# Attention, gated FFN and routed experts on one core: probabilities scaled two units ahead, biases written by ScalarE, first weights converted inside attention

## The chip, the cores and the metric

The kernel runs on one core of one Trainium2 chip. The metric is the device time of one execution in microseconds (us), the median of several runs; lower is better. Before the change it is 889.53 us, the median of 3 runs between 889.01 and 889.55.

## The reference

What has to be computed, cut to what matters here (B, H, S, D = 4, 8, 576, 64):

```python
scores = q @ k.transpose(0, 1, 3, 2) / sqrt(D)
rel = pos[:, None] - pos[None, :]
mask = (rel >= 0) & (rel < 128)                     # a window of 128 keys
scores = where(mask, scores - slopes[h] * abs(rel), -1e9)   # a bias of its own for each head
attn = exp(scores - scores.max(-1));  attn /= attn.sum(-1) + 1e-9
x = (attn @ v) as 2304 tokens x 512

gate = 1 / (1 + exp(-(x @ w_gate)))                 # w_gate, w_val: 512 x 1536, float64
x = gate * (x @ w_val) @ w_out                      # w_out: 1536 x 512, float64

# then every token goes to one of 8 experts (relu FFN, 512 -> 1024 -> 512), times its gate
```

The result is float32. In the FFN the kernel splits each operand into a high part (a copy in the type fp32r) and the rest, and adds three products (high x high, high x low, low x high).

## The kernel before

**Units of attention.** 18 blocks of 128 tokens are cut into chunks of 2, 4, 4, 4 and 4 blocks. A unit is two heads times two blocks of queries; there are 36. Each unit passes through four functions:

- `unit_s`: TensorE multiplies queries with keys into two PSUM banks (line 216). For each head and block VectorE adds the bias and takes the row's minimum in one instruction (226; the score is kept negated), and ScalarE writes exponentials and their row sum (229).
- `unit_n`: VectorE forms the reciprocals of the four sums (239, 240). Four instructions scale the probabilities by them (`scale_rows`, 108): on GpSimd, but for units 0 and 1 every second one on VectorE.
- `unit_t`: TensorE transposes the scaled probabilities (256), and VectorE and ScalarE copy them to SBUF (`hi_copy`).
- `unit_b`: TensorE multiplies them with the values (289), and the result is copied into the tile `xf` of the chunk.

`bias_of` (148) writes a head's bias, 128 x 256, the first time that it is asked for; `make_edge` copies a bias and puts a large negative number where a block holds the border of a batch. Both run on GpSimd.

**The first loop** (units 0 to 20, `NA = 20`) stands in a stretch whose order on TensorE, VectorE and ScalarE is that of the code; GpSimd's order is left to the scheduler. In pass i the code makes the edges of unit i+5, transposes unit i, scales unit i+1, multiplies unit i-1 with its values and asks for the scores of unit i+3. The table `AT` adds further work to single passes: loading the FFN's first weights, converting them, and building the operands of its token side.

**Operands of the FFN.** The FFN's two input products run as a scheme of seven products for two pairs of chunks of 512 tokens (`PAIRS`), with sums and differences of blocks in place of the eighth; the first 256 tokens (`rest`) run plainly. The token side needs A11, A12, A22 and S1 to S4. `S1+` and its like form a sum (`sum_x`, 305), and `S1` and its like split an operand: ScalarE casts the high part (96), VectorE subtracts it (112). The weight side comes in 12 blocks f. `load_w` fetches the float64 words, `conv_w` turns them into float32 (ScalarE 116, VectorE 122 to 125), `sum_w` forms four differences (354 to 357), and `split_w` casts and subtracts as above, once for the four blocks of weights (z = 0) and once for the four differences (z = 1). Converted weights go to DRAM too, from where `load_wt` fetches them for the second pair.

**The second loop** (units 20 to 35) fixes the order of TensorE alone. Between the parts of a unit it runs steps of the first pair's products, 9 for each block f (m1 to m7, and rg and rv of the rest columns), as many in a unit as `STEPS` says. Each step is followed by a part of the next block's conversion: `after` loads block f+2 behind m1, and behind later steps converts, differences and splits block f+1. Block 0's own `sum_w` and `split_w` stand ahead of the loop (530, 531, 534), with A12 and S4.

**The seam and the second pair.** What is left of the first pair's steps runs four at a time, and after each four one operand of the second pair is built (`seam`). Then the second pair's weights of block 0 are split, and S2, S3, A22 and S4 are built between its first products. In each of its blocks `split_wo(f)` also converts a block of the output weights, which come in use in the next stage. Operands, weights and converted weights all live in one pool `bpool` of 33 tiles (`slot`); a tile comes free when its last reader is done. A second pool, `op_`, of 8 tiles of the same size, is opened when attention's pool is closed, and holds the output weights.

Of the kernel before, what the change touches and what calls it, by code (L numbers as in the profile page):

```python
# [10 lines left out]
F32R = mybir.dt.float32r  # L11
# [4 lines left out]
ALU = mybir.AluOpType  # L16
# [32 lines left out]
UB = 5  # L49
STEPS = [2, 3, 4, 4] + [5] * 12  # L50


@with_exitstack
def attn_ffn_moe(ctx: ExitStack, tc: tile.TileContext, qd, kd, vd, wgv, w_out, emb, tau, w1, w2, cst, ids, out):
# [93 lines left out]
    def bias_of(h):  # L148
        while len(bias_t) <= h:
            z = len(bias_t)  # L150
            if z % 4 == 0:
                bias_c.append(slot([P, 4, 256], F32, f"bias{z}"))
            t = bias_c[-1][:, z % 4, :]
            nc.gpsimd.tensor_scalar(out=t, in0=relm, scalar1=-8.0 * 2.0 ** (-8.0 * (z + 1) / H), scalar2=0.0,
                                    op0=ALU.mult, op1=ALU.add)
            bias_t.append(t)
        return bias_t[h]
# [203 lines left out]
    def load_wt(f):  # L361
        if f < KF:
            for z, (d, src) in enumerate(((wf, wf_d), (tf, tf_d))):
                d[f] = slot([P, 2 * KD, P], F32, f"wt{z}_{f}")
                nc.sync.dma_start(flat(d[f]), src[f * P:(f + 1) * P, :])

    def split_w(pair, f, z):
        if f < KF:
            t = (wf, tf)[z].pop(f)
            h_, l_ = (slot([P, 2 * KD, P], F32R, f"w{y}{pair}{z}_{f}") for y in "hl")  # L370
            hi_copy("a", h_, t)
            lo_sub("v", l_, t, h_)
            for q, name in enumerate((("B11", "B21", "B12", "B22"), ("T1", "T2", "T3", "T4"))[z]):
                wq[pair, f, name] = (h_[:, 2 * q:2 * q + 2], l_[:, 2 * q:2 * q + 2])
# [102 lines left out]
    def latest(*engines):  # L477
# [5 lines left out]
        5: [lambda: split_x("rest", xf.pop((0, 0)))],  # L483
        12: [bA["S1+"]], 13: [bA["A22"], lambda: load_w(0)], 14: [bA["S1"]], 15: [lambda: conv_w(0, 0)],
        16: [lambda: conv_w(0, 1), lambda: load_w(1)], 17: [bA["S3+"], bA["A11"]],
        18: [bA["S2+"], bA["S3"]], 19: [bA["S2"]],
    }
    with tc.manual_schedule(engines={ENG.PE, ENG.DVE, ENG.Activation}):
        for _ in range(NWARM):
# [6 lines left out]
        unit_s(2)  # L496
        load_qk(6)
        for i in range(NA + 1):
            make_edge(i + 5)
            if i < NA:  # L500
                unit_t(i)
                unit_n(i + 1)
            if i:
                unit_b(i - 1)()
                load_v(i + 3)
            if i < NA:
                unit_s(i + LEAD)
                load_qk(i + LEAD + 4)
            for t in AT.get(i, []):
                t()  # L510
# [3 lines left out]
    for f in range(KF):  # L514
        s = seven(0, f, "mmm", True)
        steps = [s["m1"], s["m2"], s["m5"], s["m6"], s["rg"], s["m7"], s["rv"], s["m4"], s["m3"]]
        after = {0: lambda f=f: load_w(f + 2), 1: lambda f=f: conv_w(f + 1, 0), 3: lambda f=f: conv_w(f + 1, 1),
# [11 lines left out]

    sum_w(0)  # L530
    split_w(0, 0, 0)
    bA["A12"]()
    bA["S4+"]()
    split_w(0, 0, 1)
    bA["S4"]()
    late = None
    with tc.manual_schedule(engines={ENG.PE}):
        for i in range(NA, NU):
# [4 lines left out]
            unit_t(i)  # L543
            unit_n(i + 1)
            run(n // 2)
# [65 lines left out]
    bB = builds(1)  # L611
    seam = ["A11", "A12", "S1+", "S1"]
    while todo:
        run(4)
        if seam:
            bB[seam.pop(0)]()
        elif seam is not None:
            load_wt(0)
            seam = None
    split_w(1, 0, 0)  # L620
    split_w(1, 0, 1)
    load_wt(1)
    load_wo(0)

    sv = [seven(1, f, "mts", False) for f in range(KF)]
    sv[0]["m1"]()
    bB["S2+"]()
    bB["S2"]()
    sv[0]["m2"]()
    bB["S3+"]()  # L630
    bB["S3"]()
    for f in range(KF):
# [16 lines left out]
        s["m4"]()  # L649
        split_wo(f)  # L650
        load_wo(f + 1)
        s["m3"]()
        if f == 7:
            load_emb()
        elif f == 9:
            norm_emb()
        elif f == 10:
            turn_emb()


# [484 lines left out]
```

## Time and profile before

| | |
|---|---|
| median of 3 runs | 889.53 us (889.01 to 889.55) |
| the profiled execution | 888.35 us, its span 886.5 us |
| TensorE, matmul (PE) | 836.4 us busy, 94% of the span, 4616 instructions |
| TensorE, weight load (PEld) | 662.1 us, 75% |
| VectorE (DVE) | 553.1 us, 62%, 1367 instructions |
| ScalarE (ACT) | 457.0 us, 52%, 929 instructions |
| GpSimd (POOL) | 174.7 us, 20%, 283 instructions |
| mean granted TensorE clock | 0.978 of full speed |
| DMA | 140.40 MB, 158 GB/s in the mean |

The span is the time between the first and the last instruction that the profiler recorded, and the 1.85 us beside it belong to the execution too. Busy time is a mean over stages, so that it says little by itself: TensorE is at 94% over the whole, but attention's first loop lies in the first 110 us, and there it is another picture. The page's slices of 22 us show it:

```profile
PE   5987779999999889999999999999999999999997
PEld 2654457777788777777777777777878989888785
DVE  3676787878676678778855554553764555454553
ACT  4657577666664456655645555444534344233331
POOL 7443345421200000000000000022131212311210
PEclk8899799999999989999999999999999999999999
```

Each digit is the busy share of one of 40 equal slices in tenths, 9 for 90% or more; PEclk is the clock that TensorE was granted. PE stands below 9 in the first six slices, in slices 14 and 15, and in the last. How to read rows of the timeline: start and duration in us, engine, line, operation, output <- inputs, shapes, number of instructions in a row (xN), and in square brackets how long the engine had stood idle and whose result ended it.

### The profile page before, as it was taken

To read this page: it belongs to the slowest core of one execution; us is meant where nothing else is said; L and a number is where in the kernel's file an instruction comes from. 1 tells how busy PE (TensorE), PEld (TensorE's weight loads), DVE (VectorE), ACT (ScalarE), POOL (GpSimd) and SP (SyncE) were. 2 spreads that over 40 slices of the span, in tenths; PEclk is the share of its full clock that TensorE was granted. 3 is DMA by queue.
4 is the path that set the end of the run, shared out by engine and by line. 5 is a ranking of instruction groups with operands and counts; after the bars stand their busy time and mean duration, and the time that the engine had idled before them with its cause. 6 is when DMAs were issued, how large, how long until landed. Compare 5 with 4: busy or idle time off the path is not lost. (4 is left out here: it accounts for less than half of the span.)

```text
span 886.5 us, 13502 instructions
## 1 busy us (share of the span) xinstructions
PE 836.4 (94%) x4616; PEld 662.1 (75%) x4616; DVE 553.1 (62%) x1367; ACT 457.0 (52%) x929; POOL 174.7 (20%) x283
## 2 busy tenths in 40 slices
PE   5987779999999889999999999999999999999997
PEld 2654457777788777777777777777878989888785
DVE  3676787878676678778855554553764555454553
ACT  4657577666664456655645555444534344233331
POOL 7443345421200000000000000022131212311210
PEclk8899799999999989999999999999999999999999
DMA  5435446665353345665754445514265635434520
GB/s 171 120 119 168 155 163 199 228 212 182 134 197 115 121 184 196 225 222 202 238 178 119 120 143 145 158 54 132 72 191 187 219 138 196 166 114 164 180 91 17
DMA packets 72456, 140.40 MB, mean 158 GB/s; under 512 B 8984, under 2 KB 38296, under 8 KB 72386
## 3 DMA queue, kind: packets, MB, share of 16 engines
q1 hardware_dynamic: 68482, 129.41, 44.7%
q0 software_dynamic: 3904, 10.12, 3.6%
q8 instruction: 37, 0.61, 0.3%
q14 instruction: 33, 0.27, 0.1%
HBM read 103.23 MB, written 36.93 MB: 158 GB/s over the span
## 5 line engine op out<-in xcount | busy, mean ns | idle before, releaser
L722 PE MATMUL y<-wo,gh 128*128 128x512 f32 x432 | 141.4, 402 | 0.0
L902 PE MATMUL h<-xe,weh 128*128 128x256 f32 (+4 forms) x512 | 105.9, 301 | 1.6 <-DVE h L905 1.6
L108 POOL TENSOR_SCALAR p<-p,rs 128x256 f32<-128x256 f32 (+1 forms) x140 | 77.7, 572 | 139.5 <-DVE rs L240 98.1
L918 PE MATMUL z<-weh,h 128*128 128x512 f32 (+3 forms) x320 | 103.1, 399 | 0.0
L229 ACT ACTIVATE p<-p,mx 128x256 f32<-128x256 f32 (+1 forms) x144 | 69.8, 486 | 55.4 <-DVE mx L226 55.4
L722 PEld LDWEIGHTS y<-wo,gh 128*128 128x128 f32 x432 | 79.9, 188 | 20.4 <-issue 3.3
L112 DVE TENSOR_TENSOR wel<-wer,weh 128x1024 fp32r<-128x1024 f32 x64 | 78.1, 1223 | 20.6 <-ACT weh L96 20.4
L902 PEld LDWEIGHTS h<-xe,weh 128*128 128x128 f32 x512 | 83.2, 188 | 4.3 <-DVE h L905 3.0
L722 PE MATMUL y<-wo,gl 128*128 128x512 f32 x216 | 85.9, 398 | 0.0
L902 PE MATMUL h<-xe,wel 128*128 128x256 f32 (+4 forms) x256 | 76.2, 299 | 0.3 <-DVE wel L112 0.2
L904 ACT ACTIVATE h<-h 128x256 fp32r<-128x256 f32 (+4 forms) x64 | 26.6, 417 | 96.1 <-PE h L902 94.3
L96 ACT CAST weh<-wer 128x1024 fp32r<-128x1024 f32 x64 | 66.2, 1047 | 8.8 <-DMA wer<-in_w 8.8
L256 PE MATMUL t<-cs,p 128*128 128x128 f32 x272 | 48.8, 302 | 21.3 <-POOL p L108 20.4
L918 PEld LDWEIGHTS z<-weh,h 128*128 128x128 f32 (+3 forms) x320 | 56.7, 180 | 15.0
L918 PE MATMUL z<-wel,h 128*128 128x512 f32 (+3 forms) x160 | 63.1, 394 | 0.0
L256 PEld LDWEIGHTS t<-cs,p 128*128 128x128 f32 x272 | 31.7, 148 | 40.1 <-POOL p L108 36.1
L923 POOL DMA_INDIRECT out<-y,cols x19 | 25.1, 1321 | 172.1 <-DVE y L922 161.2
L905 DVE SCALAR_TENSOR_TENSOR h<-h,h 128x256 fp32r<-128x256 f32 (+4 forms) x64 | 29.6, 464 | 37.8 <-ACT h L904 37.4
L922 DVE TENSOR_SCALAR y<-z,xg 128x512 f32<-128x512 f32 (+3 forms) x22 | 16.5, 749 | 57.1 <-PE z L918 53.8
L738 ACT ACTIVATE xr<-y 128x512 f32<-128x512 f32 x18 | 10.8, 598 | 79.5 <-PE y L722 79.5
L816 POOL DMA_INDIRECT tab_d<-ids_sb,ai x18 | 18.2, 1014 | 166.4 <-DVE ai L813 144.3
L902 PEld LDWEIGHTS h<-xe,wel 128*128 128x128 f32 x256 | 48.0, 188 | 0.7 <-DVE wel L112 0.7
(327 smaller groups left out, 1953.1 us busy)
## 6 DMA issues: line engine op xcount, KB each, us to landing
wer<-in_w SPq DMA_DIRECT2D x64, 512.0 KB, 4.6
gl<-gT_d SPq DMA_DIRECT2D x27, 512.0 KB, 6.1
wr<-in_wgv SPq DMA_DIRECT2D x24, 512.0 KB, 5.5
gT_d<-c SPq DMA_DIRECT2D x48, 256.0 KB, 2.1
k<-in_kd SPq DMA_DIRECT2D x32, 192.0 KB, 3.1
v<-in_vd SPq DMA_DIRECT2D x32, 192.0 KB, 2.4
wf_d<-wf SPq DMA_DIRECT2D x12, 512.0 KB, 2.9
tf_d<-tf SPq DMA_DIRECT2D x12, 512.0 KB, 2.7
```

The lines of the kernel that those rows point to most:

```text
L96: nc.scalar.copy(o, i)
L108: nc.gpsimd.tensor_scalar(out=t, in0=t, scalar1=r, scalar2=0.0, op0=ALU.mult, op1=ALU.add)
L112: e.tensor_tensor(out=o, in0=i, in1=h.bitcast(F32), op=ALU.subtract)
L229: nc.scalar.activation(out=p[:, z, f:], in_=p[:, z, f:], func=AF.Exp, scale=-1.0, bias=mx[:, z:z + 1], accum_out=su[:, z:z + 1])
L256: nc.tensor.transpose(t[:, a:a + P], p[:, 2 * u + j, o:o + P], ident)
L722: nc.tensor.matmul(m, g[:, k % 4, u * P:(u + 1) * P], w[:, k % 3, :], start=(k == 0 and z == 0), stop=(k == KF - 1 and z == 2))
L816: nc.gpsimd.indirect_dma_start(out=tab_d, out_offset=IOA(ap=ai[:, u:u + 1], axis=0), in_=ids_sb[:, t:t + 1], in_offset=None)
L902: nc.tensor.matmul(m[:, :n], w[:, fs], x[:, k, :], start=(cnt == 0), stop=(cnt == 3 * KD - 1))
L904: nc.scalar.activation(out=hh, in_=m[:, :n], func=AF.Relu)
L905: nc.vector.scalar_tensor_tensor(out=hl, in0=m[:, :n], scalar=0.0, in1=hh.bitcast(F32), op0=ALU.max, op1=ALU.subtract)
L918: nc.tensor.matmul(m[0:w, :], h, ww[:, ds], start=(cnt == 0), stop=(cnt == 3 * KE - 1))
L923: nc.gpsimd.indirect_dma_start(out=out, out_offset=IOA(ap=idx[0:w], axis=0), in_=y[0:w, :], in_offset=None, bounds_check=NT - 1, oob_is_er ...
```

## The change

Six things are done.

- In the first loop `unit_n` runs for unit i+2 instead of i+1, behind `unit_b` and no longer right behind `unit_t`; `unit_n(1)` stands ahead of the loop. `make_edge` stands behind `unit_n`. GpSimd's order is now that of the code too. The second loop also scales unit i+2.
- `bias_of` writes biases with ScalarE.
- In `AT`, block 0's weights are loaded in pass 13 as before, but converted in passes 14 and 15, differenced in 16 and split in 17 and 18; S3 and S2 stand in passes 18 to 20. The lines of this work ahead of the second loop go.
- `STEPS` gives unit 21 four steps and unit 23 five. Block 0 runs its steps in the order m1 m5 rg m6 rv m7 m2 m4 m3.
- `wide` puts the first pair's split weights of blocks 10 and 11 into the pool `op_`.
- The last nine steps of the first pair carry the second pair's operands A11, A12, S1 and S2, and its first weights; `split_wo` comes one block later.

```diff
 UB = 5
-STEPS = [2, 3, 4, 4] + [5] * 12
+STEPS = [2, 4, 4, 5] + [5] * 12
 ...
             t = bias_c[-1][:, z % 4, :]
-            nc.gpsimd.tensor_scalar(out=t, in0=relm, scalar1=-8.0 * 2.0 ** (-8.0 * (z + 1) / H), scalar2=0.0,
-                                    op0=ALU.mult, op1=ALU.add)
+            nc.scalar.mul(t, relm, -8.0 * 2.0 ** (-8.0 * (z + 1) / H))
             bias_t.append(t)
 ...
+    def wide(shape, name, early=False):
+        return slot(shape, F32R, name) if early else op_.tile(shape, F32R, tag="c", name=name)
+
     def split_w(pair, f, z):
 ...
             t = (wf, tf)[z].pop(f)
-            h_, l_ = (slot([P, 2 * KD, P], F32R, f"w{y}{pair}{z}_{f}") for y in "hl")
+            h_, l_ = (wide([P, 2 * KD, P], f"w{y}{pair}{z}_{f}", pair or f < 10) for y in "hl")
             hi_copy("a", h_, t)
 ...
         5: [lambda: split_x("rest", xf.pop((0, 0)))],
-        12: [bA["S1+"]], 13: [bA["A22"], lambda: load_w(0)], 14: [bA["S1"]], 15: [lambda: conv_w(0, 0)],
-        16: [lambda: conv_w(0, 1), lambda: load_w(1)], 17: [bA["S3+"], bA["A11"]],
-        18: [bA["S2+"], bA["S3"]], 19: [bA["S2"]],
+        12: [bA["S1+"]], 13: [bA["A22"], lambda: load_w(0)], 14: [bA["S1"], lambda: conv_w(0, 0)],
+        15: [lambda: conv_w(0, 1), lambda: load_w(1)], 16: [lambda: sum_w(0)],
+        17: [bA["A11"], lambda: split_w(0, 0, 0)], 18: [bA["S3+"], lambda: split_w(0, 0, 1)],
+        19: [bA["S3"], bA["S2+"]], 20: [bA["S2"]],
     }
-    with tc.manual_schedule(engines={ENG.PE, ENG.DVE, ENG.Activation}):
+    with tc.manual_schedule(engines={ENG.PE, ENG.DVE, ENG.Activation, ENG.Pool}):
         for _ in range(NWARM):
 ...
         load_qk(6)
+        unit_n(1)
         for i in range(NA + 1):
-            make_edge(i + 5)
             if i < NA:
                 unit_t(i)
-                unit_n(i + 1)
             if i:
 ...
             if i < NA:
+                unit_n(i + 2)
+                make_edge(i + 5)
                 unit_s(i + LEAD)
 ...
         s = seven(0, f, "mmm", True)
-        steps = [s["m1"], s["m2"], s["m5"], s["m6"], s["rg"], s["m7"], s["rv"], s["m4"], s["m3"]]
+        steps = [s[z] for z in "m1 m2 m5 m6 rg m7 rv m4 m3".split()]
+        if f == 0:
+            steps = [s[z] for z in "m1 m5 rg m6 rv m7 m2 m4 m3".split()]
         after = {0: lambda f=f: load_w(f + 2), 1: lambda f=f: conv_w(f + 1, 0), 3: lambda f=f: conv_w(f + 1, 1),
 ...
-    sum_w(0)
-    split_w(0, 0, 0)
     bA["A12"]()
     bA["S4+"]()
-    split_w(0, 0, 1)
     bA["S4"]()
 ...
             unit_t(i)
-            unit_n(i + 1)
+            unit_n(i + 2)
             run(n // 2)
 ...
     bB = builds(1)
-    seam = ["A11", "A12", "S1+", "S1"]
-    while todo:
-        run(4)
-        if seam:
-            bB[seam.pop(0)]()
-        elif seam is not None:
-            load_wt(0)
-            seam = None
+    run(len(todo) - 9)
+    load_wt(0)
+    for t in ("A11", "A12", "S1+", "S1", "S2+"):
+        run(1)
+        bB[t]()
     split_w(1, 0, 0)
+    run(2)
+    bB["S2"]()
     split_w(1, 0, 1)
+    run(2)
     load_wt(1)
 ...
     sv[0]["m1"]()
-    bB["S2+"]()
-    bB["S2"]()
     sv[0]["m2"]()
 ...
         s["m4"]()
-        split_wo(f)
+        if f:
+            split_wo(f - 1)
         load_wo(f + 1)
 ...
             turn_emb()
+    split_wo(KF - 1)
```

What moves on the engines, as it stands in their instruction streams, at three places. A row is an instruction, and xN at its end says that there are N like it.

First the start of the program, on GpSimd and on ScalarE. The names are those of the program: `p_130`, `p_150` and `p_184` are the probabilities of units 0, 1 and 2, `rs` their reciprocal sums, and `edge` the biases with a border. On GpSimd before:

```order
L154 TENSOR_SCALAR bias_133<-cs 128x256 x4
L154 TENSOR_SCALAR bias_187<-cs 128x256 x2
L100 TENSOR_SCALAR edge_0_202<-bias_133 128x256 x2
L202 MEMSET edge_0_202 64x192
L202 MEMSET edge_0_202 128x64
L100 TENSOR_SCALAR edge_2_207<-bias_133 128x256 x2
L202 MEMSET edge_2_207 64x192
...
L202 MEMSET edge_2_308 128x64
...
L108 TENSOR_SCALAR p_130<-p_130,rs_171 128x256 x2
```

After:

```order
L108 TENSOR_SCALAR p_130<-p_130,rs_171 128x256 x2
L108 TENSOR_SCALAR p_150<-p_150,rs_202 128x256 x2
L108 TENSOR_SCALAR p_184<-p_184,rs_221 128x128
L108 TENSOR_SCALAR p_184<-p_184,rs_221 128x256
L108 TENSOR_SCALAR p_184<-p_184,rs_221 128x128
L108 TENSOR_SCALAR p_184<-p_184,rs_221 128x256
L100 TENSOR_SCALAR edge_0_228<-bias_133 128x256
L201 MEMSET edge_0_228 64x192
```

The eight biases are gone from the queue, and the scalings of the first three units stand ahead of the first edge.

On ScalarE at the same place, where `su` are the row sums and `mx` the rows' minima, before:

```order
L229 ACTIVATE p_130,su_132<-p_130,mx_131 128x128
L229 ACTIVATE p_130,su_132<-p_130,mx_131 128x256
L229 ACTIVATE p_130,su_132<-p_130,mx_131 128x128
L229 ACTIVATE p_130,su_132<-p_130,mx_131 128x256
L229 ACTIVATE p_150,su_152<-p_150,mx_151 128x128
```

After:

```order
L154 ACTIVATE bias_133<-cs 128x256
L228 ACTIVATE p_130,su_132<-p_130,mx_131 128x128
L228 ACTIVATE p_130,su_132<-p_130,mx_131 128x256
L154 ACTIVATE bias_133<-cs 128x256
L228 ACTIVATE p_130,su_132<-p_130,mx_131 128x128
L228 ACTIVATE p_130,su_132<-p_130,mx_131 128x256
L154 ACTIVATE bias_133<-cs 128x256
```

A bias now stands ahead of the two exponentials of each head.

Second, VectorE in passes 16 to 18 of the first loop. `tf` are the differences of the weights, `wl` and `xl` the low parts of weights and of the token side. Before, in these passes and behind the masks of unit 22 (`p_1302`):

```order
L305 TENSOR_TENSOR xq_(0, 'S3')_1196<-xf_0_497,xf_0_931 128x1024
L112 TENSOR_TENSOR xl_(0, 'A11')_1199<-xf_0_931,xh_(0, 'A11')_1198 128x1024
L98 COPY tt_1_1215<-t_1_1214 128x512
L239 TENSOR_SCALAR rs_1221<-su_1121 128x4
L240 RECIPROCAL rs_1221<-rs_1221 128x4
...
L305 TENSOR_TENSOR xq_(0, 'S2')_1259<-xq_(0, 'S1')_901,xf_0_931 128x1024
L112 TENSOR_TENSOR xl_(0, 'S3')_1262<-xq_(0, 'S3')_1196,xh_(0, 'S3')_1261 128x1024
L98 COPY tt_1_1273<-t_1_1272 128x256
...
L112 TENSOR_TENSOR xl_(0, 'S2')_1318<-xq_(0, 'S2')_1259,xh_(0, 'S2')_1317 128x1024
L354 TENSOR_TENSOR tf_1338<-wf_1072 128x256
L355 TENSOR_TENSOR tf_1338<-wf_1072 128x256
L356 TENSOR_TENSOR tf_1338<-wf_1072,tf_1338 128x256
L112 TENSOR_TENSOR wl_0_1345<-wf_1072,wh_0_1344 128x1024
```

After:

```order
L353 TENSOR_TENSOR tf_1150<-wf_1027 128x256
L354 TENSOR_TENSOR tf_1150<-wf_1027 128x256
L355 TENSOR_TENSOR tf_1150<-wf_1027,tf_1150 128x256
L356 TENSOR_TENSOR tf_1150<-wf_1027,tf_1150 128x256
...
L112 TENSOR_TENSOR xl_(0, 'A11')_1210<-xf_0_931,xh_(0, 'A11')_1209 128x1024
L112 TENSOR_TENSOR wl_0_1214<-wf_1027,wh_0_1213 128x1024
L98 COPY tt_1_1225<-t_1_1224 128x512
L238 TENSOR_SCALAR rs_1241<-su_1196 128x4
L239 RECIPROCAL rs_1241<-rs_1241 128x4
...
L304 TENSOR_TENSOR xq_(0, 'S3')_1274<-xf_0_497,xf_0_931 128x1024
L112 TENSOR_TENSOR wl_0_1277<-tf_1150,wh_0_1276 128x1024
L98 COPY tt_1_1288<-t_1_1287 128x256
```

The differences and both subtractions of block 0's weights stand between the masks of units 19 to 21 instead of behind those of unit 22.

Third, ScalarE around the conversion of the first pair's block 11 (`wf_3351` before, `wf_3337` after; `wr` are the words as loaded). Before:

```order
L427 COPY c_10_3407<-a_10_3333 128x512
L116 ACTIVATE wf_3351<-wr_3218 128x512
L116 ACTIVATE wf_3351<-wr_3220 128x512
L432 ACTIVATE c_10_3434<-a_10_3333 128x512
L96 CAST wh_11_3410<-wf_3351 128x1024
L96 CAST wh_11_3438<-tf_3395 128x1024
L410 COPY c_11_3458<-a_11_3451 128x512
```

After:

```order
L412 COPY c_9_3208<-a_9_3201 128x512
L418 ACTIVATE c_9_3208<-c_9_3208 128x512
L96 CAST wh_11_3392<-wf_3337 128x1024
L425 COPY r_9_3241<-a_9_3201 128x512
L454 ACTIVATE sg_9_3261<-r_3248 128x256
L96 CAST wh_11_3420<-tf_3377 128x1024
L429 COPY c_9_3275<-a_9_3201 128x512
```

The two casts of block 11's weights stood behind the last copies of block 10, right ahead of block 11's own; now they stand among the steps of block 9.

## Rows read from the trace of the kernel before

**Rows 1.** Stretches: busy us (count) of PE, PEld, DVE, ACT, POOL; PEclk; DMA share; GB/s.

```profile
0.00:22.00 22.00, 11.38 (x51) 5.77 (x51) 8.02 (x49) 9.21 (x34) 16.04 (x55) 0.90 0.57 172
...
73.00:110.00 37.00, 27.20 (x176) 16.45 (x174) 24.64 (x88) 21.77 (x71) 13.21 (x28) 0.82 0.51 162
110.00:122.00 12.00, 7.21 (x44) 4.67 (x41) 10.40 (x19) 9.39 (x18) 7.56 (x8) 0.86 0.28 94
```

**Rows 2.** Waits of TensorE, 0 to 450 us: us, count, longest.

```profile
PE t L256 <- POOL p L108: 20.4, 11, 4.3
...
PE a L383 <- ACT wh L96: 8.1, 2, 4.3
```

**Rows 3.** Timeline of TensorE, transposes of units 0, 1, 7 and 14.

```profile
14.38 1.33 PE L256 MATMUL t<-cs,p 128*128 128x128 f32 x5 [3.50 <-POOL p L108]
...
22.04 1.33 PE L256 MATMUL t<-cs,p 128*128 128x128 f32 x5 [4.35 <-POOL p L108]
...
47.23 2.05 PE L256 MATMUL t<-cs,p 128*128 128x128 f32 x8 [2.96 <-POOL p L108]
...
74.14 1.80 PE L256 MATMUL t<-cs,p 128*128 128x128 f32 x8 [0.57 <-POOL p L108]
```

**Rows 4.** Timeline of all engines, the first biases, mask and exponentials.

```profile
4.97 2.39 POOL L154 TENSOR_SCALAR bias<-cs 128x256 f32<-128x256 f32 x6 [4.02 <-DMA cs<-in_cst]
...
6.34 0.29 DVE L226 CUSTOM_DVE_ANT_0 p<-s,bias 128x128 f32<-128x128 f32 x1 [1.20 <-POOL bias L154]
...
6.67 0.40 ACT L229 ACTIVATE p<-p,mx 128x128 f32<-128x128 f32 x1 [4.66 <-DVE mx L226]
...
7.56 0.39 ACT L229 ACTIVATE p<-p,mx 128x128 f32<-128x128 f32 x1
```

**Rows 5.** Groups by shape, 20 to 110 us: busy, mean ns, idle before.

```profile
L229 ACT ACTIVATE p<-p,mx 128x256 f32<-128x256 f32 x64 | 31.8, 498 | 28.7 <-DVE mx L226 28.7
L108 POOL TENSOR_SCALAR p<-p,rs 128x256 f32<-128x256 f32 x66 | 30.6, 479 | 46.0 <-DVE rs L240 28.6 <-ACT p L229 6.8 <-PE o L289 5.1
...
L96 ACT COPY xf<-o 128x256 f32<-128x256 f32 x8 | 2.9, 367 | 3.0 <-PE o L289 3.0
...
L112 DVE TENSOR_TENSOR xl_rest<-xf,xh_rest 128x1024 fp32r<-128x1024 f32 x1 | 1.2, 1226 | 2.0 <-ACT xh_rest L96 2.0
...
L96 ACT CAST xh_rest<-xf 128x1024 fp32r<-128x1024 f32 x1 | 1.0, 1031 | 0.0
```

**Rows 6.** Timeline of VectorE, masks of unit 15, of unit 22, a split.

```profile
70.26 0.43 DVE L226 CUSTOM_DVE_ANT_0 p<-s,bias 128x256 f32<-128x256 f32 x1 [0.97 <-PE s L216]
...
79.28 0.42 DVE L226 CUSTOM_DVE_ANT_0 p<-s,bias 128x256 f32<-128x256 f32 x1
...
82.58 1.23 DVE L112 TENSOR_TENSOR xl_(0, 'S1')_1017<-xq_(0, 'S1')_901,xh_(0, 'S1')_1016 128x1024 fp32r<-128x1024 f32 x1 [2.10 <-ACT xh_(0, 'S1')_1016 L96]
...
84.57 0.42 DVE L226 CUSTOM_DVE_ANT_0 p<-s,bias 128x256 f32<-128x256 f32 x1
...
109.54 0.42 DVE L226 CUSTOM_DVE_ANT_0 p<-s,bias 128x256 f32<-128x256 f32 x1 [1.87 <-PE s L216]
```

**Rows 7.** Timeline of GpSimd, the scalings from 111 us on.

```profile
111.29 7.56 POOL L108 TENSOR_SCALAR p<-p,rs 128x256 f32<-128x256 f32 x8 [1.59 <-ACT p L229]
```

**Rows 8.** Timeline of TensorE, the first products of blocks 0.

```profile
115.24 0.50 PE L383 MATMUL a<-xh_(0, 'A11')_1198,wh 128*128 128x512 f32 x1 [3.79 <-ACT wh L96]
...
121.57 0.50 PE L383 MATMUL b<-xh_(0, 'A12')_1348,wh 128*128 128x512 f32 x1
```

**Rows 9.** Timeline of TensorE, the first products of block 11.

```profile
312.13 0.80 PE L383 MATMUL a<-xh_(0, 'A11')_1198,wh 128*128 128x512 f32 x1 [4.29 <-ACT wh L96]
...
318.16 0.39 PE L383 MATMUL c<-xh_(0, 'S1')_1016,wh 128*128 128x512 f32 x1
...
319.55 0.39 PE L383 MATMUL a<-xh_(0, 'S2')_1317,wh 128*128 128x512 f32 x1
```

**Rows 10.** Timeline of ScalarE, the conversion of block 11.

```profile
306.35 1.23 ACT L116 ACTIVATE wf<-wr 128x512 f32<-128x512 f32 x2 [2.06 <-PE a L383]
```

## The prediction

> **What bounds the kernel now.** I read the table of stretches first, then who TensorE waited for, then TensorE, VectorE, ScalarE and GpSimd in order of time through the first 135 us and around 310 us. From 132 us on TensorE hardly waits, with one hole at 308; so the change can only be worth what TensorE loses ahead of 132 us and in that hole. In the first 22 us it is busy for 11.4, from 73 to 110 for 27.2 of 37, from 110 to 122 for 7.2 of 12 [rows 1]. What it waited for is mostly two things: the scaled probabilities from GpSimd, 20.4 us in 11 waits, and the cast weights from ScalarE, 8.1 us in 2 waits [rows 2].
>
> **Start, units 0 to 3.** The transposes of unit 0 wait 3.50 us and those of unit 1 4.35 us for GpSimd [rows 3]. Both times the wanted scalings stand behind biases and edge masks: GpSimd's first six biases alone take 2.39 us from 4.97 on [rows 4]. Now the scalings come first on GpSimd, and ScalarE writes the biases. No ScalarE bias is in the trace; the nearest rows are a copy of the same shape, 0.37 us, and an exponential, 0.50 us [rows 5]. I take 0.37, since a bias has no accumulator. What it costs is an alternation: bias h+1 stands behind the exponentials of head h, and the mask of head h+1 waits for it. A head's two exponentials take 0.89 us (6.67 to 7.56), a mask reaches its exponential in 0.33 us (6.34 to 6.67) [rows 4]: 0.89 + 0.37 + 0.33 = 1.59 us a head, eight heads in the first four units. The first bias ends at 4.97 + 0.37, its mask starts at about 5.5, the first exponential at 5.85. The mask of head 5 then ends at some 14.0; the sums of unit 1 stand behind it (0.35 us), two GpSimd scalings of 0.48 [rows 5] end at 15.4, and unit 1 is transposed from about 15.7 instead of 22.04 [rows 3]. That is -6.3 us. With biases of 0.50 us the eight cost 1 us more, and every other delay on that chain stays under a microsecond: -4.5 at worst. At best also the wait of the first mask for its bias, 1.20 us [rows 4], goes fully: -7.8.
>
> **Units 5 to 11.** The split of the rest columns holds up VectorE, and unit 7 waits 2.96 us for its scalings and unit 14 0.57 us [rows 3]. With scalings two units ahead TensorE does not stand at them. Late next are the copies of the transposes, behind the same subtraction: mask 1.4 us, wait for the cast to 3.4, subtraction to 4.6, copy to 5.2, against a TensorE unit of about 3.7 us ((74.14 - 47.23 - 0.57) / 7 [rows 3]). The two waits make 3.5 us; I leave 1.1 of them: -2.4, between 0 and -3.5.
>
> **Units 12 to 19.** Here the lead does not help by itself: VectorE's own queue sets the pace. The masks of unit 15 start at 70.26, those of unit 22 at 109.54 [rows 6]: 39.3 us for seven units, where TensorE needs 26. In a unit with a split VectorE sits 2.1 us until ScalarE has cast, subtracts 1.23 us, copies, and only then masks: 5.3 us from 79.28 to 84.57 [rows 6]. The change puts more here: two subtractions of 1.23 us [rows 5] for the first block's weights and the four differences, together as many columns as one subtraction, 1.3 us by estimate: +3.8. It gives back one cast wait of 2.1 us, because two splits now share a unit, and the 1.87 us that VectorE waited at 109.54 for late scores [rows 6]: -0.2. The two extra casts, 1.03 us each [rows 5], run beside a subtraction. I take -0.5; if nothing is given back it is +3.8, and if the conversion hides entirely in cast waits -4.
>
> GpSimd's scalings cross these subtractions. Eight of them took 7.56 us from 111.29 [rows 7], 0.95 us each against 0.48 alone [rows 5], while VectorE ran operations with two inputs. In two units' lead even 3.8 us a unit is hidden on GpSimd; on VectorE I book nothing here and price it as a rival. The Trainium skill (SBUF — State Buffer, section Who interferes with whom) says that a VectorE instruction with two SBUF inputs and a GpSimd instruction that reads SBUF exclude each other, and that the one issued second waits for the whole of the other. By that rule the loss could as well be VectorE's, the engine that sets the pace here; the stretched scalings agree that one of the two waits, and show it on GpSimd.
>
> **First products.** After the masks of unit 22 TensorE gets to its second product group only at 121.57, 12.0 us later, with 3.79 us waiting for the first cast weights at 115.24 [rows 6, 8]. Its own work there is a unit (3.7), a quarter unit more and six products; six products take 1.39 us at full speed (318.16 to 319.55 [rows 9]): 6.0 us. Now both halves of the weights are converted two units earlier. What is late next is S2, behind S3 on both engines; with m5 and the rest product put ahead of m6, TensorE has some 7 us before it asks. -6.0, less 1 for products at the lower clock after the idle stretch before (0.82 and 0.86 of full, between the levels of 1.2 and 2.4 GHz [rows 1]): -5.0, between -2.5 and -6.5. The larger early steps ask for block 1 sooner; VectorE has about 18.5 us of work before it, TensorE 20, so I book nothing, and -2.5 holds a microsecond or two there.
>
> **Hole at 308.** Block 11 waits 4.29 us for its cast weights and then runs its first twelve products from 312.13 to 318.16 [rows 9], twice as long as at full speed (2.8 us). Its conversion began at 306.35 because it waited for a TensorE product to free a buffer [rows 10]. With blocks 10 and 11 in the other pool the conversion waits for no product, and its casts stand in block 9's time. From the end of block 10 (312.13 - 4.29 = 307.84) to 318.16 are 10.3 us against 2.8: -7.5, between -4.3 (the low clock stays) and -7.6. Late next would be the second pair's S3, A22 and S4, built behind block 11; three casts and three subtractions, under 7 us, beside eight product groups, 11 us.
>
> **Tail.** Output weights are split one block later, so two conversions stand at the end of the second pair, where TensorE has no spare group. The trace of before does not show it; one cast and one subtraction, 2.3 us [rows 5], bound it, nothing is the other end. Blocks 10 and 11 of them are used last in the next stage: +0.3, between 0 and +1.5. Moved loads go through SyncE in nearly the old order: nothing.
>
> **Sum.** -6.3 - 2.4 - 0.5 - 5.0 - 7.5 + 0.3 = -21.4 us. The profiled execution took 888.35 us, its span 886.5; 888.35 - 21.4 = 867.0. It lies 1.2 us under the median of 889.53, so I say 867.5. The likeliest's own range is 862 to 872.
>
> **Rivals.**
> VectorE pays (0.18). For: the crossing scalings [rows 7] and a VectorE that is never ahead in units 13 to 19. Against: the scalings start with the masks, which read PSUM, and are mostly done before the subtractions. Price: 28 scalings of 0.48 us at worst 13.4 us, half of them 6.7: 888.4 - 21.4 + 6.7 + 1 = about 874.5.
> The second hole stays (0.12): the first load or cast of the second pair, or S3, comes late in place of block 11. For: six more operands and two weight blocks are built in the same 25 us; against: block 0 of the second pair is cast in block 10's time. The -7.5 goes: 875.
> ScalarE eats the start (0.08): biases of 0.5 us, and masks, exponentials and copies of four units in lockstep to 24 us. For: ScalarE is then without a gap; against: 8 x 1.59 is 12.7 us only. -6.3 goes: 873.5.
> Slower (0.04): the sums two units ahead wait for exponentials just issued, and VectorE's in-order queue stands at them, so that masks, exponentials, sums and copies run one after another: 4 x 0.50 + 0.5 for the exponentials, 0.35 sums, 1.1 copies, 0.95 scores, nearly 4.9 us a unit against 3.7. Over twenty units +24: 888.4 - 21.4 + 24 = 891. From 4.8 us a unit it decides. Against: the copies stand ahead of the sums, and the scores of the next unit do not wait for them, so the wait covers work that is due anyway: about 2.9 us a unit.
>
> **Chances.** Forecast 0.50, the rivals 0.18, 0.12, 0.08 and 0.04; 0.05 for more than the forecast gives (all lower bounds together -29.3: 859); 0.03 for several rivals at once, ending within 0.2%, about what a measurement of this kernel can tell from no change. Faster by over 0.2%: 0.93; slower: 0.04. The range 858 to 880 leaves out the slower case and the combinations.
>
> **What would show it.** Unit 1's transposes near 16 us and no TensorE wait on GpSimd over 1 us; masks of unit 22 some 9 us earlier, near 100; the first product within 4 us of those masks; no wait for block 11's weights, and the clock at 1.00 through 290 to 310. The forecast is wrong if units 12 to 19 take over 43 us, if TensorE stands at the start of the second pair, or if it waits in the stage after 440 for output weights.

## The result, and the profile after

The changed kernel takes 865.5 us (median of 4 runs, 864.99 to 866.54) against 889.51 for the kernel before: ratio 0.9733, 95% interval 0.9716 to 0.9750. The forecast was 867.5 (858 to 880). The total was right. Of its six terms three hold in mechanism (the start, the first products, of which most is lost again later, and the hole at 308), and the experiments show what stood in place of the others.

The stretches of the changed kernel, in the columns of [rows 1]:

```profile
0.00:22.00 22.00, 16.87 (x72) 9.64 (x72) 9.91 (x55) 12.46 (x43) 6.00 (x20) 0.77 0.59 173
...
73.00:110.00 37.00, 28.90 (x186) 20.25 (x186) 28.75 (x87) 25.66 (x76) 18.89 (x36) 0.82 0.54 169
110.00:122.00 12.00, 10.09 (x72) 7.88 (x74) 11.79 (x28) 9.29 (x23) 8.55 (x12) 1.00 0.56 173
```

TensorE is busier in each of them, yet from 73 to 110 us VectorE's 28.75 of 37 and TensorE's 28.90 stand side by side, and in the next 12 us VectorE is at 11.79. What TensorE waited for up to 450 us (us, times, longest), against [rows 2]:

```profile
PE t L255 <- ACT tt L96: 6.9, 9, 2.4
PE a L385 <- ACT r L425: 4.1, 3, 2.1
PE t L255 <- DVE rs L238: 4.0, 5, 1.2
...
PE t L255 <- POOL p L108: 0.3, 1, 0.3
```

The 20.4 us of waiting for GpSimd's scalings are 0.3 now, and the 8.1 for cast weights are gone. In their place stand the copies of the transposes, VectorE's queue and ScalarE's copy of a product (line 425), 15 us in these three.

Where the time goes is best read from landmarks: the same row of work, looked up in both timelines of TensorE. Before: the transposes of units 12 and 20, then the first products of blocks 1 and 10, of the second pair, and of the experts.

```profile
66.72 0.33 PE L256 MATMUL t<-cs,p 128*128 128x128 f32 x1
110.36 0.33 PE L256 MATMUL t<-cs,p 128*128 128x128 f32 x1
141.06 0.47 PE L383 MATMUL a<-xh_(0, 'A11')_1198,wh 128*128 128x512 f32 x1
294.93 0.39 PE L383 MATMUL a<-xh_(0, 'A11')_1198,wh 128*128 128x512 f32 x1
327.90 0.39 PE L383 MATMUL a<-xh_(1, 'A11')_3151,wh 128*128 128x512 f32 x1
623.60 0.36 PE L902 MATMUL h<-xe,weh 128*128 128x256 f32 x1
```

After, with unit 1's transposes (22.04 before [rows 3]) ahead of them:

```profile
17.64 1.54 PE L255 MATMUL t<-cs,p 128*128 128x128 f32 x6
56.44 0.33 PE L255 MATMUL t<-cs,p 128*128 128x128 f32 x1
97.11 0.33 PE L255 MATMUL t<-cs,p 128*128 128x128 f32 x1
124.24 0.39 PE L385 MATMUL a<-xh_(0, 'A11')_1209,wh 128*128 128x512 f32 x1
282.30 0.39 PE L385 MATMUL a<-xh_(0, 'A11')_1209,wh 128*128 128x512 f32 x1
307.57 0.39 PE L385 MATMUL a<-xh_(1, 'A11')_3446,wh 128*128 128x512 f32 x1
600.41 0.36 PE L905 MATMUL h<-xe,weh 128*128 128x256 f32 x1
```

The changed kernel is ahead by 4.4 us at unit 1, 10.3 at unit 12, 13.3 at unit 20, 16.8 at block 1, only 12.6 at block 10, 20.3 at the second pair and 23.2 at the experts; the spans differ by 23.4.

Three cautions on these numbers. A landmark comes from one execution: the first mask starts between 6.42 and 7.54 us in the changed kernel and the seven variants with the same start, so that differences under about 1 us mean nothing here unless the start is allowed for. Unit 1's first transpose ran at 17.22 before, and the row at 22.04 is that of the other five. And the new `STEPS` move steps ahead of attention's work: at block 1 the changed kernel has not yet transposed unit 23 (1.03 us), so that like for like it is 15.8 us ahead there; at block 2, with unit 25 in the same place, it is 11.8 (147.08 against 159.87, less 1.03). From block 9 on attention is done in both.

### The profile page after: what moved, and what is told of

It is laid out like the page before. It is cut to its first block, busy times and chain, and to the rows that moved or that the text cites. A ratio compares the mean times of both kernels' runs of the same rounds, so it can differ in the third digit from the quotient of the medians.

```text
span 863.1 us, 13488 instructions
## 1 busy us (share of the span) xinstructions
PE 824.4 (96%) x4616; PEld 663.7 (77%) x4616; DVE 552.7 (64%) x1367; ACT 459.7 (53%) x937; POOL 174.9 (20%) x275
## 5 line engine op out<-in xcount | busy, mean ns | idle before, releaser
L108 POOL TENSOR_SCALAR p<-p,rs 128x256 f32<-128x256 f32 (+1 forms) x140 | 81.4, 600 | 131.5 <-DVE rs L239 72.9
L725 PEld LDWEIGHTS y<-wo,gh 128*128 128x128 f32 x432 | 79.9, 188 | 20.3 <-issue 3.3
L255 PE MATMUL t<-cs,p 128*128 128x128 f32 x272 | 41.6, 294 | 13.6 <-ACT tt L96 6.9
L215 PE MATMUL s<-k,q 64*128 64x256 f32 (+1 forms) x288 | 46.1, 428 | 3.9 <-DVE mx L225 3.9
```

The costliest lines, as they stand in the source:

```text
L108: nc.gpsimd.tensor_scalar(out=t, in0=t, scalar1=r, scalar2=0.0, op0=ALU.mult, op1=ALU.add)
L215: nc.tensor.matmul(ss[u][:, j * 256 + f:j * 256 + 256], q[halves[u], j * P:(j + 1) * P], k[halves[u], j * P + f:j * P + 256], start=True, ...
L255: nc.tensor.transpose(t[:, a:a + P], p[:, 2 * u + j, o:o + P], ident)
L725: nc.tensor.matmul(m, g[:, k % 4, u * P:(u + 1) * P], w[:, k % 3, :], start=(k == 0 and z == 0), stop=(k == KF - 1 and z == 2))
```

## The experiments

Each ratio is to the kernel before on the same chip; the changed kernel's is 0.9733. A difference of two ratios times 889 us gives the us between two variants; since each interval is about 0.0017 to either side, differences under some 2 us are not told apart. All but the last two undo or alter a part of the changed kernel.

**Scalings one unit ahead.**

```diff
+                unit_n(i + 1)          # behind unit_t(i), in both loops
-                unit_n(i + 2)
```

> The changed kernel (865.5 us) with one part undone: scalings one unit ahead again, in both loops; GpSimd's fixed order, ScalarE's biases and all else stay. Theory (the lead itself takes away TensorE's waits for GpSimd in units 5 to 20): waits of 2 to 3 us come back at units 7, 15, 16 and 19, 4 to 8 us in all: 870 to 873. Rival (the gain there came from GpSimd's order and from work that moved, VectorE sets the pace in any case): 865 to 867.

Measured: 876.37 us, ratio 0.9855 (0.9838 to 0.9871): the lead is worth 10.9 us, more than either theory said. The waits came back at the units named, but with 15.5 us in 10 waits for GpSimd instead of the 4 to 8 expected, and the granted clock from 73 to 110 us fell from 0.82 to 0.70. The rest stands in no wait of TensorE's products, but in those of its weight loads. Groups by shape from 22 to 73 us, where the loads (PEld) of the transposes bring in the probabilities; before:

```profile
L256 PEld LDWEIGHTS t<-cs,p 128*128 128x128 f32 x95 | 10.9, 151 | 18.0 <-POOL p L108 17.3
L256 PE MATMUL t<-cs,p 128*128 128x128 f32 x95 | 19.8, 314 | 8.0 <-POOL p L108 7.5
```

the changed kernel:

```profile
L255 PEld LDWEIGHTS t<-cs,p 128*128 128x128 f32 x104 | 11.1, 141 | 11.2 <-issue 7.0 <-POOL p L108 2.0 <-POOL edge L201 1.8
L255 PE MATMUL t<-cs,p 128*128 128x128 f32 x104 | 14.5, 278 | 6.3 <-ACT tt L96 4.5 <-DVE tt L98 0.9 <-DVE rs L238 0.9
```

and this run:

```profile
L255 PEld LDWEIGHTS t<-cs,p 128*128 128x128 f32 x96 | 9.9, 140 | 16.4 <-POOL p L108 15.8
L255 PE MATMUL t<-cs,p 128*128 128x128 f32 x96 | 19.3, 296 | 5.4 <-POOL p L108 4.3 <-ACT tt L96 0.4
```

With one unit's lead the loads wait 16 to 17 us for GpSimd in these 51 us, and the products' rows show 4 to 8 of them: the others are gaps inside rows, too short to be listed. One unit of the kernel before shows them, eight loads in pairs:

```profile
55.83 0.20 PEld L256 LDWEIGHTS t<-cs,p 128*128 128x128 f32 x2 [0.56 <-POOL p L108]
56.25 0.20 PEld L256 LDWEIGHTS t<-cs,p 128*128 128x128 f32 x2 [0.21 <-POOL p L108]
56.70 0.20 PEld L256 LDWEIGHTS t<-cs,p 128*128 128x128 f32 x2 [0.25 <-POOL p L108]
57.15 0.20 PEld L256 LDWEIGHTS t<-cs,p 128*128 128x128 f32 x2 [0.26 <-POOL p L108]
```

and a unit of the changed kernel at the same time:

```profile
56.44 0.86 PEld L255 LDWEIGHTS t<-cs,p 128*128 128x128 f32 x8 [0.33 <-issue]
```

Before, TensorE transposed in step with GpSimd's four scalings, which loses 0.6 to 0.7 us in a unit that shows a wait of 0.19 us or none. The clock is not in this: it was 1.00 from 55.5 to 58 us of the kernel before.

**Biases on GpSimd in program order.**

```diff
-            nc.scalar.mul(t, relm, -8.0 * 2.0 ** (-8.0 * (z + 1) / H))
+            nc.gpsimd.tensor_scalar(out=t, in0=relm, scalar1=..., scalar2=0.0,
```

> The changed kernel with the biases on GpSimd again, at the places in its fixed order where the program asks for them. Theory (it was the queue: scalings that stood behind biases and edges that were not yet due): the first four biases are written by 6.6 us and no scaling waits for them, and ScalarE loses eight instructions of 0.40 us from its alternation with the exponentials: 862 to 865. Rival (the move to ScalarE was needed): units 1 to 3 are scaled 2 to 4 us later, 867 to 870.

Measured: 866.70 us, 0.9747 (0.9730 to 0.9763), short of both ranges and not told apart from the changed kernel. Unit 1 was transposed at 14.24 us instead of 17.64, but unit 2 at 22.97 instead of 22.18, because the mask of the seventh head stood behind four edges on GpSimd. VectorE's timeline shows the wait:

```profile
19.71 0.29 DVE L226 CUSTOM_DVE_ANT_0 p<-s,bias 128x128 f32<-128x128 f32 x1 [5.09 <-POOL bias L154]
```

So it is the queue that matters, but GpSimd's queue in that order has a hole of its own.

**Block 0 converted after attention.**

```diff
-        15: [lambda: conv_w(0, 1), lambda: load_w(1)], 16: [lambda: sum_w(0)],
-        17: [bA["A11"], lambda: split_w(0, 0, 0)], 18: [bA["S3+"], lambda: split_w(0, 0, 1)],
+        # the table, the lines ahead of the second loop and block 0's order as before
```

> The changed kernel with the first block's conversion at its old places (differences and both splits behind the first loop), the old table of extra work and the old order of block 0's steps. Theory (converting earlier pays because the first products need not wait): TensorE waits 3 to 4 us for the first cast weights and again before the differences, VectorE gets back some of it in units 12 to 19: 868 to 871. Rival (VectorE's work is the same wherever it stands, and VectorE sets the pace until 132 us): 865 to 866.5.

Measured: 866.44 us, 0.9737 (0.9716 to 0.9758): no difference, the rival's number. The wait that the theory names did come back:

```profile
103.46 0.80 PE L385 MATMUL a<-xh_(0, 'A11')_1205,wh 128*128 128x512 f32 x1 [3.88 <-ACT wh L96]
```

This execution started 0.9 us later than the changed kernel's (18.55 at unit 1). Less that, it is 0.9 us ahead at unit 20 (97.16 against 97.11), so that much the moved work costs in units 12 to 19; 3.9 us behind at block 1 (129.06), where the step numbers are the same in both; and 1.8 behind at block 2 (149.84 against 147.08), at block 8 (259.93 against 257.21) and at the second pair (310.31). The earlier conversion does what it should at block 0, and 2.1 us of it are given back in block 1.

**Blocks 10 and 11 in the common pool; the old seam; both.**

```diff
-            h_, l_ = (wide([P, 2 * KD, P], f"w{y}{pair}{z}_{f}", pair or f < 10) for y in "hl")
+            h_, l_ = (wide([P, 2 * KD, P], f"w{y}{pair}{z}_{f}", True) for y in "hl")    # first, third
-    for t in ("A11", "A12", "S1+", "S1", "S2+"):
-        run(1)
-        bB[t]()
+    seam = ["A11", "A12", "S1+", "S1"]                                      # second, third
+    while todo:
+        run(4)
 ...                                                                     # the rest of the old seam
```

> The changed kernel with the first pair's split weights of blocks 10 and 11 back in the common pool. Theory (the hole ahead of block 11 came from the pool alone): the conversion of block 11 waits for a buffer again, TensorE stands some 4 us and runs twelve products at half clock: 872 to 873.5. Rival (the second pair's operands, built later one by one, had already made room): 865 to 867.

> The changed kernel with the second pair's operands built as before (one for each four steps, S2 behind the second pair's first product). Theory (the order at the seam only makes room; the pool of blocks 10 and 11 carries the gain): no wait over 1 us, 865 to 867. Rival (half of the gain at block 11 is the seam's): waits of 3 to 5 us between 295 and 330 us, 869 to 873.

> The changed kernel with both parts around block 11 undone: its split weights and those of block 10 in the common pool, and the second pair's operands built in the old places. Undone one at a time, neither brought the hole back. Theory (either of the two makes enough room in the common pool, so that each hides the other's worth): the conversion of block 11 waits for a TensorE product again, TensorE stands some 4 us and runs at half clock behind it: 871.5 to 873.5. Rival (the hole went for a third reason, the earlier conversion or the new lead): 864 to 866.5.

Measured: 864.88 us with the pool undone (0.9726, 0.9710 to 0.9742), 864.32 with the seam undone (0.9724, 0.9708 to 0.9740), 873.71 with both (0.9827, 0.9809 to 0.9845). Neither alone costs anything, both together 8.4 us. In the run with both undone TensorE stands at block 11 and goes on at half pace (granted clock 0.50 from 300.7 to 306 us),

```profile
300.71 0.80 PE L385 MATMUL a<-xh_(0, 'A11')_1209,wh 128*128 128x512 f32 x1 [4.55 <-ACT wh L96]
```

because ScalarE's conversion waits for a product to free a buffer, as in [rows 10]:

```profile
294.94 1.22 ACT L116 ACTIVATE wf<-wr 128x512 f32<-128x512 f32 x2 [2.33 <-PE a L385]
```

Each edit frees the common pool enough by itself.

**Old numbers of steps; output weights in their own block.**

```diff
+STEPS = [2, 3, 4, 4] + [5] * 12     # first
+        split_wo(f)                 # second: not f - 1
```

> The changed kernel with the old numbers of steps in units 21 and 23 (3 and 4 for 4 and 5). The changed kernel's lead over the kernel before shrinks from 16.8 us at block 1 to 12.6 us at block 8, with a wait of 2.12 us for ScalarE at 136.6 us and half clock behind it. Theory (the two more steps ask too much of ScalarE and VectorE in blocks 0 and 1): 862.5 to 865. Rival (the loss is that of the denser stretch itself, and two steps fewer only leave more for later): 865 to 867.

> The changed kernel with the output weights split in their own block again, not one later. I had put the delay at +0.3 us; the traces have the last block of the second pair some 1.4 us shorter instead, where the kernel before waits 0.65 and 0.73 us for ScalarE's copies. Theory (the delay took those waits away): 866.5 to 867.5. Rival (they went for another reason): 865 to 866.

Measured: 866.71 us (0.9755, 0.9736 to 0.9774) and 863.42 (0.9725, 0.9708 to 0.9741), the second below both of its ranges, but neither told apart from the changed kernel. Both theories fall. The steps are not what loses the lead: with the old numbers 5.1 us of it go between units 21 and 22 (107.24 and 120.83 against 123.06 and 131.53 before). The output weights' delay costs nothing and brings nothing that can be told apart, and the waits at the tail stay away without it; what fills them stands under Tail below.

**Four biases ahead of the first mask; all eight first on GpSimd.**

```diff
+        bias_of(3)                  # first: ScalarE, ahead of unit_s(0)
-            nc.scalar.mul(t, relm, -8.0 * 2.0 ** (-8.0 * (z + 1) / H))           # second
+            nc.gpsimd.tensor_scalar(out=t, in0=relm, scalar1=..., scalar2=0.0,   # second
 ...
+        bias_of(H - 1)              # second: ahead of unit_s(0)
```

> The changed kernel with the first four heads' biases written ahead of the first mask, where ScalarE stands idle from 5.3 to 7.0 us. Theory (the alternation of bias, mask and exponentials sets the pace of the first units, 1.66 us a head): the next three heads take about 1.1 us each, unit 1 is transposed 1.5 to 2 us earlier and all that follows with it: 863 to 864. Rival (VectorE's queue in units 12 to 19 takes it back): 865 to 866.

> The changed kernel with all eight biases on GpSimd, ahead of everything else there, where it stands idle until 10 us: neither ScalarE's alternation (8 x 0.40 us) nor the wait of 5.09 us that the run with GpSimd's biases in program order had for the seventh bias. Theory (the place of the biases matters, not the engine): unit 2 is transposed near 18 us instead of 22.2, 860 to 862. Rival (what is gained at the start is lost at VectorE's queue in units 12 to 19): 864 to 866.

Measured: 861.62 us (0.9687, 0.9665 to 0.9710) and 858.89 (0.9662, 0.9646 to 0.9678). In the first, unit 1 is transposed at 15.22, 2.4 us earlier, and the ratio gives 4.1 us, good to some 3: the theory holds, and its rival falls short. The second is the fastest version, 6.3 us below the changed kernel. GpSimd's timeline of it, and TensorE's at units 1 and 2:

```profile
4.98 3.37 POOL L154 TENSOR_SCALAR bias<-cs 128x256 f32<-128x256 f32 x8 [4.03 <-DMA cs<-in_cst]
```

```profile
13.81 0.87 PE L256 MATMUL t<-cs,p 128*128 128x128 f32 x6 [0.44 <-ACT tt L96]
...
16.84 0.84 PE L256 MATMUL t<-cs,p 128*128 128x128 f32 x6 [0.29 <-POOL edge L202]
```

All eight biases are written by 8.4 us, when GpSimd has nothing else to do. Unit 2 starts at 16.84 against 22.18 in the changed kernel, 5.3 us earlier. Of this lead 3.8 us stand at unit 20 (93.27 against 97.11) and 3.5 at block 1, but 5.1 again at block 2 and at the second pair: what VectorE's stretch holds back is regained in block 1 (21.24 us against 22.84).

**Parts alone on the kernel before.**

```diff
+                unit_n(i + 2)       # the lead and GpSimd's order; first and second
+                make_edge(i + 5)
+        bias_of(H - 1)              # second only, and wide() as in the change
```

> The kernel before (889 us) with one part of the change alone: scalings two units ahead in both loops, and GpSimd's order that of the code; biases stay on GpSimd. Theory (the lead is worth the same wherever it stands, 11 us, since TensorE no longer goes at the pace of GpSimd's four scalings in each unit; GpSimd's order adds some 3 to 4 us at the start): 873 to 877. Rival (the 11 us need the other parts, above all the earlier conversion): 880 to 885.

> The kernel before with three parts: scalings two units ahead with GpSimd in code order, all eight biases first on GpSimd, and the split weights of blocks 10 and 11 in the other pool. Left out are the earlier conversion of block 0, the new numbers and order of steps, the new seam and the later output weights. Theory (these parts carry all that can be measured): 861 to 864. Rival (the parts left out, each too small to measure alone, add up to some microseconds, and the tail's waits of 1.4 us stay): 865 to 869.

Measured: 878.87 us (0.9891, 0.9874 to 0.9907) and 861.97 (0.9703, 0.9686 to 0.9719). The lead alone falls between the theory and its rival: 12.3 us ahead of the kernel before at unit 20 (98.03), 10.7 at the first product (104.51), 9.7 in all. At block 0 it waits 4.14 us for the first cast weights and 0.93 us more, as the kernel before does [rows 8]. The three parts of the second run carry 26.4 of 30 us: the best version is 0.41% below it, 3.6 us, so that the parts left out do add up to something, of which 1.8 us stand at the second pair's first product (304.19 against 302.43) and 1.4 are the two waits at the tail (0.65 and 0.73 us), which this run has as the kernel before does. The time is in the theory's range, but the theory's words, that these parts carry all that can be measured, fall, and the rival's sentence on the tail holds.

## Why the prediction was right, and where not

**Start, -6.3.** Measured -4.4 at unit 1, at the edge of the range of this term, with a landmark's 1 us to either side. The alternation on ScalarE is there: VectorE's masks of the first heads, the second and third behind a bias each,

```profile
6.65 0.29 DVE L225 CUSTOM_DVE_ANT_0 p<-s,bias 128x128 f32<-128x128 f32 x1 [1.58 <-PE s L215]
...
8.31 0.29 DVE L225 CUSTOM_DVE_ANT_0 p<-s,bias 128x128 f32<-128x128 f32 x1 [1.01 <-ACT bias L154]
...
9.97 0.29 DVE L225 CUSTOM_DVE_ANT_0 p<-s,bias 128x128 f32<-128x128 f32 x1 [1.01 <-ACT bias L154]
```

1.66 us a head against 1.59 worked out, a bias 0.40 against 0.37. What I missed is the first mask: it waits for TensorE's scores (1.58 us), not for its bias, and so starts at 6.65 instead of 5.5. The 1.1 us there and five times 0.07 make most of the difference. (The term's best end, -7.8, was also more than its parts: 6.3 and 1.2 make 7.5.) The best version shows what the alternation itself costs: the queue on GpSimd had to be sorted, not emptied.

**Units 5 to 11, -2.4 between 0 and -3.5.** Here the prediction failed: 5.9 us were won between units 1 and 12, 4.8 of them from unit 5 on (31.43 against 36.91 us). The step that fails is the bound, "The two waits make 3.5 us": I summed the listed waits of the products, and took for TensorE's own pace a unit of 3.7 us that had GpSimd's pace in its rows. The changed kernel passes units 9 to 12 at 3.2 us each (46.94 to 56.44). The rows of units 7 and 14 in [rows 3] say so: eight transposes in 2.05 and 1.80 us, where the changed kernel's take 1.06 to 1.09 in units 8 to 12 (part of the 2.05 is clock, 0.73 of full from 47 to 50 us).

**Units 12 to 19, -0.5.** Measured -3.0 (from 10.3 to 13.3 us ahead), inside the bounds of +3.8 and -4, but by luck: two steps fail here, with opposite signs. The first is "Here the lead does not help by itself". Of the 20.4 us of waits in [rows 2] 8.9 lie in units 15 to 19, and I gave no price to them. Units 12 and 20 of the kernel before with the lead alone, and of the changed kernel without the lead:

```profile
59.16 0.33 PE L256 MATMUL t<-cs,p 128*128 128x128 f32 x1
98.03 0.33 PE L256 MATMUL t<-cs,p 128*128 128x128 f32 x1
...
64.39 0.33 PE L255 MATMUL t<-cs,p 128*128 128x128 f32 x1
111.21 0.46 PE L255 MATMUL t<-cs,p 128*128 128x128 f32 x1
```

The lead alone takes these eight units from 43.6 us to 38.9, and without it the changed kernel takes 46.8 for them instead of 40.7: 4.8 to 6.1 us for a term that I had put at nothing. The second is the cost of the moved conversion, +3.8 less 4.0 given back, which makes -0.2 and not -0.5: measured +0.9 us, by the run that undoes it. With the lead in place TensorE waits for copies and for VectorE instead.

**First products, -5.0.** The wait for the first cast weights is gone, as forecast, and the second product group starts at 104.24 us against 121.57 [rows 8], 17.3 ahead with the same work behind it: measured -4.1 from unit 20, inside the range. Then 4.7 are lost again by block 10, 4.0 of them in block 1 (15.8 to 11.8 like for like), which I had booked at nothing ("VectorE has about 18.5 us of work before it, TensorE 20"). In block 1 TensorE comes to stand behind the conversion of block 2's weights. Its wait, and the cast on ScalarE ahead of it:

```profile
136.62 0.50 PE L385 MATMUL a<-xh_(0, 'S3')_1332,wh 128*128 128x512 f32 x1 [2.12 <-ACT r L425]
...
133.07 1.05 ACT L96 CAST wh<-tf 128x1024 fp32r<-128x1024 f32 x1 [1.58 <-DVE tf L356]
```

ScalarE's copy of the product stands behind this cast and four exponentials. The cast waited 1.58 us for the last of the weights' differences, which stood behind a weight subtraction on VectorE (131.49 to 132.70), and the exponentials follow it without a gap. The granted clock was 0.72 from 136 to 140 us. The run without the earlier conversion puts the net of it at 0.4 us by its ratio, which is noise, and at 1.8 by the landmarks. So of the 5.5 us of these two terms under 2 are left; the rest was moved work on engines that had no time to spare.

**Hole at 308, -7.5.** Measured -7.7 (12.6 to 20.3), and 8.4 by the run with both parts undone. Size and mechanism hold: no wait for block 11's weights, and the clock at 1.00 from 280 to 340 us. But the pool need not have done it: the new seam would have done it too.

**Tail, +0.3.** Measured -2.9 from the second pair to the experts. The step that fails is "where TensorE has no spare group". The two waits of 0.65 and 0.73 us of the last block are gone, and in their place TensorE runs the first products with the output weights (`y`). Before, and after:

```profile
442.04 0.50 PE L383 MATMUL a<-xh_(1, 'S3')_3581,wh 128*128 128x512 f32 x1 [0.65 <-ACT r L423]
444.42 0.50 PE L383 MATMUL a<-xh_(1, 'A22')_3592,wh 128*128 128x512 f32 x1 [0.73 <-ACT c L427]
...
419.92 0.40 PE L725 MATMUL y<-wo,gh 128*128 128x512 f32 x1
421.33 0.39 PE L385 MATMUL a<-xh_(1, 'S3')_3581,wh 128*128 128x512 f32 x1
422.71 0.40 PE L725 MATMUL y<-wo,gh 128*128 128x512 f32 x1
```

The code fixes no order here, so this one is the scheduler's. The changed kernel and all its variants have 8 to 12 such rows ahead of the second pair's last product, and no wait over 0.5 us there; the kernel before and the two runs built on it have none ahead of it and both waits. Another 1.5 us lie in the pace of the second pair's products, 9.5 us a block against 9.7 for its first six, at a granted clock of 1.00 in both. That goes with the order too. Before, four or five products of two other groups stand between the second and the third of a block's six products with A11; after, none. So its fourth follows its first by 1.71 us (343.35 and 345.06), against 0.68 after (332.06 and 332.74). The run with the lead alone has the mixed order and 9.7, the one with three parts the straight order and 9.5; in the runs with the pool, the seam or both undone only the first block is mixed, and takes 10.0 to 10.1 where the next takes 9.5. That the order makes the pace is not tested by itself, and which part of the change moved the scheduler stays open.

So the total came out by two errors of opposite sign: the lead was worth 10.9 us and I had given it 2.4, beside 6.3 for the start; the earlier conversion, given 5.5, brought 2 at most. That they met at 865.5 us, 2 from the forecast, is luck. (With the 1.2 us that it names, the sum of 867.0 makes 868.2, not 867.5.) No rival decided. "VectorE pays" is the one that came nearest, though not by crossing scalings: VectorE's subtractions kept 1.22 to 1.23 us, all but one, and its pace shows instead in what TensorE loses again in block 1.

## What to carry to other kernels

Waits in brackets are not all of an engine's waiting: where a row groups several instructions, compare its length with the shortest row of the same shape, and look at the weight loads' waits beside the products'. An engine that writes what another reads piece by piece sets its pace without a wait that is long enough to be listed, and a lead of one more unit is then worth a piece of every unit. Work brought forward on an engine that sets the pace later mostly moves the wait, whereas work moved to an engine's idle time at the start (eight biases, 3.4 us) was kept nearly in full. Where a scheduler chooses an engine's order, compare the two orders before looking for a cause of a changed pace or a lost wait. And two edits that each cure the same shortage look worthless when undone singly, so that both have to be undone together once.

## What the runs showed of the hardware

GpSimd scales 128 x 256 in 0.41 us when alone (four in 1.64, from 56.40 in the changed kernel). Beside VectorE's two-input operations on 128 x 1024 it takes far longer; its group from 60 to 125 us of the changed kernel (count, busy us, mean ns):

```profile
L108 POOL TENSOR_SCALAR p<-p,rs 128x256 f32<-128x256 f32 x38 | 26.6, 715 | 29.5 <-DVE rs L239 27.6 <-ACT tt L96 1.8
```

Four scalings from 101.03 on took 3.90 us, beside two of these operations that fill VectorE from 101.39 to 103.75. VectorE's own, all but two, keep 1.22 to 1.23 us there. The Trainium skill (SBUF — State Buffer, section Who interferes with whom) lets whichever of the two was issued second wait for the other; in these traces it is nearly always GpSimd that pays.
